# Second mixture of a pooled-attention kernel: operand sums of a later pass made ahead, first-pass stores and sums moved back

## Chip, cores and metric

The kernel runs on one core of a Trainium2 chip. The metric is the device time of one execution in microseconds (us), as the median of several runs; lower is better. Engines are named as in the profile: PE (matmul, with PEld for its weight loads), DVE (vector), ACT (scalar), POOL (GpSimd), SP (the queue that issues most DMAs).

## What is computed

Pooled attention, a routed mixture of experts (top two of eight), and a second, dense mixture. Only the last matters here; it takes the span from about 600 us to the end.

```python
def _moe2_ref(x, w_gate, w1, w2):          # x 2304x512, E = 8, F = 1024
    logits = x @ w_gate
    P = np.exp(logits - logits.max())
    for _ in range(8):
        P /= P.sum(1, keepdims=True) + 1e-09
        P /= P.sum(0, keepdims=True) + 1e-09
        P *= N / E
    for e in range(E):
        out += P[:, e:e + 1] * (np.maximum(x @ w1[e], 0.0) @ w2[e])
```

## The kernel before

Every fp32 product is three matmuls: each operand is split into a high part `h` (an ACT copy, L153) and a low part `l` (source minus high part, on DVE or POOL, L154), and h·h, h·l, l·h are summed (L148 to L150 and L1009 to L1011). `split` does one operand, `relu_split` (L158, tiles hh and hl) one that also goes through the ReLU.

The second mixture works in three passes of 768 tokens (`NPS`). A pass has 32 steps: 8 experts by 4 quarters of F. A step multiplies by blocks in a scheme with seven products instead of eight; its operands are sums of blocks. For the right operand of layer 1, the tokens, there are seven tiles per pass, `bh0` to `bh6` and `bl0` to `bl6` (B11, B21, B22, T1 to T4), each 128x768 and held once, so a new pass overwrites the tiles that the old pass read.

First pass (steps 0 to 31): `load_w` loads w1 and w2 into r1 and r2, makes four weight sums in tile `sw` (128x256 each, L174 to L177) and splits. `keep_w` stores the split weights to DRAM (`a_d`, `b_d`). `keep_t` makes four more sums of w2 in tile `tt` (L206 to L209, on POOL), splits them whole (th on ACT, tl on DVE, 128x1024) and stores them (`t_d`). It starts with the weights of step 4; the sums of steps 0 to 3 (`back`) follow in steps 10, 14, 18 and 22, with w2 loaded once more. `first2` is layer 1 (42 matmuls 128x384), `second2` layer 2 of the step before (36 matmuls 128x512), drained on DVE into `acc` (L995, L999).

In steps 2 and 3 of the first pass `balance` runs the eight normalisations of P. It is a generator: after every second product `tick` lets PE do one small matmul (L940) on column sums `bs` that DVE has just made (L938), and the order of instructions is fixed there, so PE waits if bs is late.

Passes 2 and 3 (steps 32 to 95) fetch the stored weights (`fetch_w`). `first_w` has 42 matmuls 128x384, `left_w` makes sums and splits of the hidden blocks on POOL (tiles cl), `second_w` has 63 matmuls 128x256 (L1009 to L1011), drained into `acc`: the first value of a pass ("fresh", 12 drains) by ACT with a scale (L1115), all others by DVE (L1117). `acc` is held once; when a pass is over, six DMAs take it to `out`, and the fresh drains of the next pass must wait for them.

At a change of pass `right(ps)` makes the 14 tiles in three slices of 256 columns (`right_part`): for each slice four POOL sums into `sw` (L245 to L248) and seven splits, in the order B11, T2, T3, T1, B21, T4, B22. The tokens `xr` of the last pass are loaded by `right_raw`.

A scheduler orders the instructions of each engine ahead of time; each engine then runs its list in order.

Of the kernel before, what the change touches and what calls it, by code (L numbers as in the profile page):

```python
# [8 lines left out]
F32 = mybir.dt.float32  # L9
# [19 lines left out]
def tile_pooled_attention_moe_moe(  # L29
# [46 lines left out]
    NW = 4  # L76
    G0 = PB
# [122 lines left out]
    def keep_t(r2, e, qi, pool):  # L200
# [4 lines left out]
        G = nc.gpsimd  # L205
# [4 lines left out]
        split(th, tl, t)  # L210
# [649 lines left out]
    with ExitStack() as es:  # L860
# [13 lines left out]
        XR = {}  # L874
# [84 lines left out]

        def right(ps):  # L960
            XT[ps] = right_tiles(xb, CH)
            for i in range(PB // 2):
                right_part(ps, i)

        def right_part(ps, i):
            c = i * P, (i + 1) * P
            tx = wp.tile([P, 4, K2, P], F32, name="sw", bufs=1)
            right_t(XR[ps], tx, nc.gpsimd if ps else nc.vector, *c)
            right_split(XR[ps], tx, XT[ps], *c, [nc.vector] if ps else [nc.vector, nc.gpsimd])

# [112 lines left out]
        def second_w(ps, e, qi):  # L1083
# [18 lines left out]
            for bank, l, r, again, half, cols, new in (  # L1102
# [7 lines left out]
                for t in range(h):  # L1110
# [3 lines left out]
                    if fresh and new:  # L1114
                        nc.scalar.activation(a, bank[t], AF.Copy, scale=pe)  # L1115
                    else:
                        nc.vector.scalar_tensor_tensor(a, bank[t], pe, a, op0=ALU.mult, op1=ALU.add)  # L1117
# [22 lines left out]
        back = steps[0:4]  # L1140
        for n, (ps, e, qi) in enumerate(steps):
            if n == 3:
                yg_s.close()
                tq = tq_s.enter_context(tc.tile_pool(name="tq", bufs=1, reuse_waits="tile"))
            if n + 1 < len(steps):
# [4 lines left out]
                else:  # L1150
                    W[nx] = load_w(w1b, w2b, *nx[1:], en, en)
                    if n >= 3:
                        keep_t(W[nx][4], *nx[1:], tq)
            if ps == 0:
                keep_w(W[ps, e, qi], e, qi)
                if n >= 10 and n % 4 == 2 and back:
                    st = back.pop(0)
                    r2 = wp.tile([P, FB, DM], F32, name="r2")
                    nc.sync.dma_start(r2, w2b[st[1], st[2] * QF:(st[2] + 1) * QF, :]
                                      .rearrange("(k p) d -> p k d", p=P))  # L1160
                    keep_t(r2, *st[1:], tq)
            if e == E - 1 and qi == NQ - 2 and 1 < ps + 1 < NPS:
                right_raw(ps + 1)
# [9 lines left out]
            if ps == 0:  # L1173
                first2(ps, e, qi)
                if n:
                    second2(*steps[n - 1])
                else:
# [7 lines left out]
                    for nb in range(PB, PB + 4):  # L1185
                        combine(nb)
            elif n == E * NQ:
# [41 lines left out]
```

## Time and profile before

| | |
|---|---|
| runs | 2205.8, 2208.61, 2209.41 us (median 2208.61) |
| profiled execution | 2206.33 us, its span 2204.5 us |
| granted TensorE clock | 0.975 of full speed over the span |
| PE busy | 2088.4 us (95%) |
| DVE, POOL, ACT busy | 1535.0, 1465.1, 988.6 us |
| DMA | 489.79 MB, 222 GB/s over the span |

PE's share is near full except in a few places: until about 600 us (other layers), at 720 to 790 us (the normalisations, beside steps 2 to 4 of the first pass) and at 1680 to 1740 us (the change from the second to the third pass). A window's row gives the length and, for each engine, busy us and the number of instructions, then the granted clock, the share of DMA engines busy and GB/s. A time line's row gives the start, the duration, and in brackets the idle time before it and what ended it.

### The profile page before, as it was taken

What the parts mean: (1) busy time and instruction counts of PE and PEld (TensorE: products, weight loads), DVE (VectorE), ACT (ScalarE), POOL (GpSimd) and SP (SyncE); (2) the same over time, 40 slices, a digit from 0 to 9 for tenths busy, and PEclk for the clock granted to TensorE, in tenths of its full rate; (3) what the DMA queues carried; (4) which work ended last, traced back from release to release, by engine and by line L of the source; (5) the groups of instructions that cost most, each with busy time, mean ns of one, the idle gap of its engine ahead of it and who ended that gap; (6) DMA issues with size and microseconds to landing.
All of it is one profiled execution on the core that took longest, in us unless ns stands there. A gap on an engine that the chain in (4) does not pass through costs nothing.

```text
span 2204.5 us, 35357 instructions
## 1 busy us (share of the span) xinstructions
PE 2088.4 (95%) x12801; PEld 1951.8 (89%) x12801; DVE 1535.0 (70%) x3092; ACT 988.6 (45%) x1957; POOL 1465.1 (66%) x1390
## 2 busy tenths in 40 slices
PE   4896999999999799999999999999999999999998
PEld 3785888888989688988888999999998899999998
DVE  4686777677477677777778576666767466766766
ACT  4663444454355334343434544444444544444443
POOL 3356656554371468999995767667677677677675
PEclk9788999999999899999999999999999999999999
DMA  8535343333449767888878666766666666667664
GB/s 179 156 102 146 104 144 117 123 124 110 137 168 360 247 220 285 337 320 330 327 288 312 234 236 242 254 237 245 244 241 227 224 239 256 235 237 260 237 237 163
DMA packets 182673, 489.79 MB, mean 222 GB/s; under 512 B 21312, under 2 KB 72512, under 8 KB 182368
## 3 DMA queue, kind: packets, MB, share of 16 engines
q1 hardware_dynamic: 171664, 464.73, 59.7%
q0 software_dynamic: 7664, 21.19, 2.7%
q8 instruction: 102, 1.67, 0.3%
q10 hardware_dynamic: 3168, 1.57, 0.2%
q14 instruction: 75, 0.61, 0.1%
HBM read 348.29 MB, written 139.15 MB: 221 GB/s over the span
## 4 chain that ended last, share of the span: by engine, by line
PE 64%; POOL 8%; DVE 7%; DMA 3%; issue 3%; ACT 2%; SPq 0%; POOLq 0%; ACTq 0%; DVEq 0%
PE pb L148 7%; PE pb L149 7%; PE pb L150 7%; PE py L150 4%; PE py L148 4%; PE x L1009 4%; PE py L149 4%; PE x L1010 4%; PE ph L148 4%; PE x L1011 4%; PE ph L149 3%; PE ph L150 3%; POOL al L154 3%; DVE acc L1117 2%; PE pb L1009 1%
## 5 line engine op out<-in xcount | busy, mean ns | idle before, releaser
L1117 DVE SCALAR_TENSOR_TENSOR acc<-x,Pm,acc 128x256 f32<-128x256 f32 x750 | 340.8, 478 | 110.1 <-PE x L1011 105.4
L154 POOL TENSOR_TENSOR cl<-xg,ch 128x384 fp32r<-128x384 f32 x192 | 197.4, 1028 | 258.1 <-ACT ch L153 245.4
L148 PE MATMUL pb<-bh,ah 128*128 128x384 f32 x882 | 301.1, 342 | 9.1 <-DVE acc L1117 9.0
L149 PE MATMUL pb<-bl,ah 128*128 128x384 f32 x882 | 297.8, 338 | 0.8 <-DVE bl L154 0.8
L150 PE MATMUL pb<-bh,al 128*128 128x384 f32 x882 | 296.8, 337 | 0.0
L148 PE MATMUL py<-h,hh 128*128 128x512 f32 x704 | 278.4, 396 | 5.2 <-DVE acc L999 3.8
L149 PE MATMUL py<-l,hh 128*128 128x512 f32 x704 | 277.5, 395 | 0.0
L150 PE MATMUL py<-h,hl 128*128 128x512 f32 x704 | 265.3, 397 | 3.2 <-DVE hl L158 2.8
L148 PE MATMUL ph<-bh,ah 128*128 128x384 f32 (+1 forms) x798 | 262.1, 329 | 5.1 <-DVE hl L158 3.0
L149 PE MATMUL ph<-bl,ah 128*128 128x384 f32 (+1 forms) x798 | 260.1, 326 | 0.0
L150 PE MATMUL ph<-bh,al 128*128 128x384 f32 (+1 forms) x798 | 259.3, 326 | 0.6 <-DVE al L154 0.6
L154 POOL TENSOR_TENSOR cl<-ys,ch 128x384 fp32r<-128x384 f32 x256 | 256.7, 1024 | 2.6 <-ACT ch L153 2.6
L1117 DVE SCALAR_TENSOR_TENSOR acc<-pb,Pm,acc 128x256 f32<-128x256 f32 x318 | 151.7, 478 | 83.5 <-PE pb L1011 71.8
L148 PEld LDWEIGHTS pb<-bh,ah 128*128 128x128 f32 x882 | 167.1, 189 | 16.0 <-DVE acc L1117 15.4
L999 DVE SCALAR_TENSOR_TENSOR acc<-py,Pm,acc 128x512 f32<-128x512 f32 x168 | 124.4, 745 | 66.7 <-PE py L150 65.0
L1009 PE MATMUL x<-r,ch 128*128 128x256 f32 x576 | 162.7, 285 | 7.0 <-ACT acc L1115 4.0
L149 PEld LDWEIGHTS pb<-bl,ah 128*128 128x128 f32 x882 | 167.3, 190 | 1.1 <-DVE bl L154 1.0
L150 PEld LDWEIGHTS pb<-bh,al 128*128 128x128 f32 x882 | 166.3, 189 | 0.0
L148 PEld LDWEIGHTS ph<-bh,ah 128*128 128x128 f32 x798 | 150.7, 189 | 17.0 <-DVE hl L158 4.2
L1010 PE MATMUL x<-r,ch 128*128 128x256 f32 x576 | 161.4, 282 | 0.0
L153 ACT ACTIVATE ch<-ys 128x384 fp32r<-128x384 f32 x256 | 129.4, 518 | 68.8 <-POOL ys L1068 68.6
L148 PEld LDWEIGHTS py<-h,hh 128*128 128x128 f32 x704 | 133.0, 189 | 29.8 <-DVE acc L999 6.0
(301 smaller groups left out, 5693.3 us busy)
## 6 DMA issues: line engine op xcount, KB each, us to landing
r<-in_moe_w_dram SPq DMA_DIRECT2D x148, 512.0 KB, 4.1
r<-t_d SPq DMA_DIRECT2D x128, 512.0 KB, 6.2
ah<-a_d SPq DMA_DIRECT2D x64, 896.0 KB, 4.6
al<-a_d SPq DMA_DIRECT2D x64, 896.0 KB, 7.3
a_d<-ah SPq DMA_DIRECT2D x32, 896.0 KB, 5.8
a_d<-al SPq DMA_DIRECT2D x32, 896.0 KB, 6.1
l<-b_d SPq DMA_DIRECT2D x64, 384.0 KB, 2.9
h<-b_d SPq DMA_DIRECT2D x64, 384.0 KB
```

The lines of the kernel that those rows point to most:

```text
L148: nc.tensor.matmul(ps, lh, rh, start=first, stop=False, skip_group_check=again)
L149: nc.tensor.matmul(ps, lh, rl, start=False, stop=False, skip_group_check=again)
L150: return nc.tensor.matmul(ps, ll, rh, start=False, stop=last, skip_group_check=again)
L153: nc.scalar.activation(hi, src, AF.Copy)
L154: (en or nc.vector).tensor_tensor(lo, src, hi.bitcast(F32), op=ALU.subtract)
L999: nc.vector.scalar_tensor_tensor(a, py, pe, a, op0=ALU.mult, op1=ALU.add)
L1009: nc.tensor.matmul(ps, lh, rh, start=not again, stop=False, skip_group_check=again)
L1010: nc.tensor.matmul(ps, lh, rl, start=False, stop=False, skip_group_check=again)
L1011: nc.tensor.matmul(ps, ll, rh, start=False, stop=True, skip_group_check=again)
L1117: nc.vector.scalar_tensor_tensor(a, bank[t], pe, a, op0=ALU.mult, op1=ALU.add)
```

## The change

- `right` for passes 2 and 3: three sums (128x768) are made ahead, at steps of the last expert of the pass before (`right_sum`: T1 in `sw`, T2 in `tt` or a new tile `e1`, T3 in place in `xr`); at the change itself seven whole splits 128x768 remain, in the order B11, B21, T2, T1, T3, B22, T4, with one POOL sum for T4. For the third pass the tokens are loaded, and two of the sums stand on POOL, as early as the start of the second pass.
- `keep_t` starts with the weights of step 8 (`T0` is 7). The back sums are now eight, one in each of the steps 9 to 16, after the products of the step; they run on DVE. Every `keep_t` splits in two halves of 128x512.
- `keep_w` stands behind `first2`.
- The fresh drains move from ACT to DVE (`tensor_scalar`).

The products on PE are the same 11,830 listed instructions; POOL's list gets 48 rows shorter, ACT's 36, DVE's 51 longer.

```diff
+    T0 = 7
-    def keep_t(r2, e, qi, pool):
+    def keep_t(r2, e, qi, pool, G):
...
-        G = nc.gpsimd
...
-        split(th, tl, t)
+        for c in range(0, 4, 2):
+            split(th[:, c:c + 2], tl[:, c:c + 2], t[:, c:c + 2])
...
+        def right_sum(ps, i, pool, nm):
+            G = nc.gpsimd
+            xr = XR[ps]
+            b11, b12, b22 = xr[:, 0:K2, 0, :], xr[:, 0:K2, 1, :], xr[:, K2:KD, 1, :]
...
+            if i == 0:
+                TS[ps] = [half(wp.tile([P, 4, K2, P], F32, name="sw", bufs=1))]
+                G.tensor_tensor(TS[ps][0], b12, b11, op=ALU.subtract)
+            elif i == 1:
+                TS[ps].append(half(pool.tile([P, 3 if nm == "e1" else 4, K2, P], F32, name=nm, bufs=1)))
+                G.tensor_tensor(TS[ps][1], b22, TS[ps][0], op=ALU.subtract)
+            else:
+                G.tensor_tensor(b12, b22, b12, op=ALU.subtract)
...
         def right(ps):
             XT[ps] = right_tiles(xb, CH)
-            for i in range(PB // 2):
-                right_part(ps, i)
...
+            t1, t2 = TS.pop(ps)
+            for i, src in ((B11, b11), (B21, b21), (T2, t2), (T1, t1), (T3, b12), (B22, b22)):
+                split(*XT[ps][i], src)
+                if i == B21:
+                    nc.gpsimd.tensor_tensor(b21, b21, t2, op=ALU.subtract)
+            split(*XT[ps][T4], b21)
...
-                        nc.scalar.activation(a, bank[t], AF.Copy, scale=pe)
+                        nc.vector.tensor_scalar(a, bank[t], pe, None, op0=ALU.mult)
...
-        back = steps[0:4]
+        back = steps[0:T0 + 1]
...
-                    if n >= 3:
-                        keep_t(W[nx][4], *nx[1:], tq)
-            if ps == 0:
-                keep_w(W[ps, e, qi], e, qi)
-                if n >= 10 and n % 4 == 2 and back:
...
-            if e == E - 1 and qi == NQ - 2 and 1 < ps + 1 < NPS:
-                right_raw(ps + 1)
+                    if n >= T0:
+                        keep_t(W[nx][4], *nx[1:], tq, nc.gpsimd)
...
                 first2(ps, e, qi)
                 if n:
+                    keep_w(W[ps, e, qi], e, qi)
+                if n:
                     second2(*steps[n - 1])
...
+                if n >= T0 + 2 and back:
+                    st = back.pop(0)
...
+                    keep_t(r2, *st[1:], tq, nc.vector)
...
+            if e == E - 1 and ps + 1 < NPS:
+                if qi == 0 and ps:
+                    right_raw(ps + 1)
+                elif ps and qi:
+                    right_sum(ps + 1, (0, 2, 1)[qi - 1], hc, "e1")
+                elif qi == NQ - 1:
+                    for i in range(3):
+                        right_sum(ps + 1, i, tq, "tt")
```

DVE's list around the fourth normalisation, before (cs, Pm, rs and bs belong to the normalisation; u, s, hl and acc to the step's products; line numbers as in the profile):

```order
L942 RECIPROCAL cs<-plg 128x8
L154 TENSOR_TENSOR tl<-tt,th 128x1024
L943 SCALAR_TENSOR_TENSOR Pm<-Pm,cs 128x18x8
L158 SCALAR_TENSOR_TENSOR hl<-s_7793,hh 128x384
L995 TENSOR_TENSOR acc<-py_7806,acc 128x512
L934 TENSOR_REDUCE rs<-Pm 128x18
L995 TENSOR_TENSOR acc<-py_7825,acc 128x512
L158 SCALAR_TENSOR_TENSOR hl<-u_7734,hh 128x384
L935 RECIPROCAL rs<-rs 128x18
L936 TENSOR_TENSOR Pm<-Pm,rs 128x18x8
L938 TENSOR_REDUCE bs<-Pm 128x8
```

and now (the lines of the changed file are one higher here, 23 higher from `second2` on):

```order
L943 RECIPROCAL cs<-plg 128x8
L159 SCALAR_TENSOR_TENSOR hl<-u_7702,hh 128x384
L944 SCALAR_TENSOR_TENSOR Pm<-Pm,cs 128x18x8
L935 TENSOR_REDUCE rs<-Pm 128x18
L1018 TENSOR_TENSOR acc<-py_7780,acc 128x512
L936 RECIPROCAL rs<-rs 128x18
L937 TENSOR_TENSOR Pm<-Pm,rs 128x18x8
L1018 TENSOR_TENSOR acc<-py_7799,acc 128x512
L939 TENSOR_REDUCE bs<-Pm 128x8
```

The low-part split `tl` of `keep_t` stood between the reciprocal and the multiplication; now no row of `keep_t` stands in the whole stretch of the eight normalisations.

DVE's list in one of the steps 9 to 16, now (r is the w2 tile loaded again, tt its sums):

```order
L319 TENSOR_TENSOR s_9091<-ph,u_9056 128x384
...
L155 TENSOR_TENSOR tl<-tt,th 128x512 x2
...
L206 TENSOR_TENSOR tt<-r_8989 128x256
L208 TENSOR_TENSOR tt<-r_8989 128x256
L1022 SCALAR_TENSOR_TENSOR acc<-py_9110,Pm,acc 128x512
L207 TENSOR_TENSOR tt<-r_8989,tt 128x256
L1022 SCALAR_TENSOR_TENSOR acc<-py_9118,Pm,acc 128x512
L159 SCALAR_TENSOR_TENSOR hl<-u_9056,hh 128x384
L306 TENSOR_TENSOR u_9225<-ph,m_9216 128x384
L209 TENSOR_TENSOR tt<-r_8989,tt 128x256
L155 TENSOR_TENSOR tl<-tt,th 128x512
```

Before, such a step had one `tl` row of 128x1024 and no `tt` row on DVE; now it has the four sums and two pairs of `tl` halves, between the drains that PE waits for.

DVE's list at the change to the third pass, before (a piece of it):

```order
L154 TENSOR_TENSOR bl_18698<-sw,bh_18697 128x2x128
L1117 SCALAR_TENSOR_TENSOR acc<-x_18863,Pm,acc 128x256
L1117 SCALAR_TENSOR_TENSOR acc<-x_18864,Pm,acc 128x256
L1117 SCALAR_TENSOR_TENSOR acc<-y_18865,Pm,acc 128x256
L1117 SCALAR_TENSOR_TENSOR acc<-y_18866,Pm,acc 128x256
L154 TENSOR_TENSOR bl_18694<-sw,bh_18693 128x2x128
L154 TENSOR_TENSOR bl_18692<-sw,bh_18691 128x2x128
L154 TENSOR_TENSOR bl_18690<-sw,bh_18689 128x2x128
L154 TENSOR_TENSOR bl_18698<-sw,bh_18697 128x2x128
```

and now:

```order
L155 TENSOR_TENSOR bl_18734<-sw,bh_18733 128x768
L1056 TENSOR_TENSOR u_18573<-pb_18522,u_18547 128x384
L1140 SCALAR_TENSOR_TENSOR acc<-x_18626,Pm,acc 128x256
L1140 SCALAR_TENSOR_TENSOR acc<-x_18624,Pm,acc 128x256
L155 TENSOR_TENSOR bl_18740<-xr,bh_18739 128x768
L155 TENSOR_TENSOR bl_18738<-xr,bh_18737 128x768
L1140 SCALAR_TENSOR_TENSOR acc<-pb_18622,Pm,acc 128x256
```

PE's list there, now (x_18860 is the bank whose drains end the second pass, x_19072 the same bank in the third):

```order
L1032 MATMUL x_18860<-r_18306,ch_18595 128x256
L1033 MATMUL x_18860<-r_18307,ch_18595 128x256
L1034 MATMUL x_18860<-r_18306,cl_18596 128x256
...
L1032 MATMUL x_19072<-h_18510,ch_18821 128x256
L1033 MATMUL x_19072<-l_18511,ch_18821 128x256
L1034 MATMUL x_19072<-h_18510,cl_18822 128x256
...
L1032 MATMUL x_19072<-r_18512,ch_18845 128x256
```

The 21 slice splits on DVE, four of every seven behind a POOL sum of their slice, are seven whole ones, and only the last of them waits for a sum made at the change itself. Between the last product for x_18860 and the second use of that bank in the third pass (the last row), PE's list has 27 matmuls beside the three shown. On SP four of the six DMAs to `out` now stand together ahead of the four loads of `b_d` and `t_d`, and two behind them; before, two stood ahead, two before these loads, and two behind them.

## Rows read from the trace of the kernel before

**Rows 1.** The page: busy time, and PE's busy tenths in 40 slices.

```profile
PE 2088.4 (95%) x12801; PEld 1951.8 (89%) x12801; DVE 1535.0 (70%) x3092; ACT 988.6 (45%) x1957; POOL 1465.1 (66%) x1390
PE   4896999999999799999999999999999999999998
```

**Rows 2.** Windows: a steady stretch, then the change of pass; engines PE, PEld, DVE, ACT, POOL.

```profile
1400.00:1500.00 100.00, 99.15 (x702) 98.54 (x700) 69.29 (x160) 44.14 (x92) 73.39 (x75) 1.00 0.66 239
1680.00:1720.00 40.00, 36.25 (x217) 33.12 (x216) 27.78 (x62) 17.91 (x42) 27.32 (x29) 0.96 0.58 201
1720.00:1740.00 20.00, 15.24 (x90) 14.81 (x90) 6.35 (x14) 11.50 (x26) 14.14 (x15) 0.83 0.63 247
```

**Rows 3.** Waits of PE, 1676 to 1722 us: total, times, longest.

```profile
PE pb L148 <- DVE acc L1117: 1.0, 1, 1.0
PE pb L149 <- DVE bl L154: 0.8, 1, 0.8
```

**Rows 4.** Time line of PE, SP and ACT, 1717 to 1729 us.

```profile
1717.45 0.39 PE L1009 MATMUL x<-r,ch 128*128 128x256 f32 x1
...
1719.49 1.35 SPq L1119 DMA_DIRECT2D out_dram<-acc  x2
...
1727.58 1.21 ACT L1115 ACTIVATE acc<-x,Pm 128x256 f32<-128x256 f32 x3 [2.58 <-DMA out_dram<-acc]
...
1728.11 0.58 PE L1009 MATMUL x<-r,ch 128*128 128x256 f32 x1 [3.98 <-ACT acc L1115]
```

**Rows 5.** Windows in the stretch of the normalisations.

```profile
740.00:780.00 40.00, 30.51 (x129) 25.51 (x130) 30.18 (x67) 9.07 (x14) 16.82 (x16) 0.84 0.52 191
...
764.00:768.00 4.00, 2.61 (x7) 2.25 (x8) 3.05 (x9) 0.00 (x0) 2.79 (x4) 0.50 0.93 360
768.00:772.00 4.00, 4.00 (x15) 3.19 (x14) 2.23 (x6) 0.00 (x0) 0.00 (x0) 0.72 0.01 4
```

**Rows 6.** Waits of PE, 735 to 800 us.

```profile
PE plg L940 <- DVE bs L938: 8.8, 5, 4.8
```

**Rows 7.** Time line of DVE and PE, 738 to 766 us.

```profile
738.79 1.22 DVE L154 TENSOR_TENSOR tl<-tt,th 128x1024 fp32r<-128x1024 f32 x1 [3.83 <-ACT th L153]
...
740.72 0.37 PE L920 MATMUL plg<-ident,mx 128*1 128x128 f32 x1 [0.98 <-DVE mx L918]
...
750.81 0.31 DVE L943 SCALAR_TENSOR_TENSOR Pm<-Pm,cs 128x144 f32<-128x144 f32 x1
...
757.92 1.18 DVE L154 TENSOR_TENSOR tl<-tt,th 128x1024 fp32r<-128x1024 f32 x1
759.01 1.40 DVE L943 SCALAR_TENSOR_TENSOR Pm<-Pm,cs 128x144 f32<-128x144 f32 x1
...
764.82 0.42 DVE L938 TENSOR_REDUCE bs<-Pm 128x8 f32<-128x152 f32 x1
```

**Rows 8.** Windows of 16 us (about a step), first pass; sum and mean of 19.

```profile
949.00:965.00 16.00, 16.00 (x81) 14.37 (x81) 11.08 (x17) 5.78 (x10) 14.27 (x15) 1.00 1.02 397
...
sum 304.00, PE 301.91 PEld 271.28 DVE 231.40 ACT 116.99 POOL 278.19; mean PE 15.89 PEld 14.28 DVE 12.18 ACT 6.16 POOL 14.64
```

**Rows 9.** Waits of PE and of DVE, 800 to 1210 us.

```profile
PE py L148 <- DVE acc L999: 3.4, 4, 1.6
...
DVE acc L999 <- PE py L150: 59.9, 77, 2.1
```

**Rows 10.** Tiles th and sw: DVE's operations, durations min/median/max in ns.

```profile
L154 DVE TENSOR_TENSOR tl<-tt,th x32: 1180/1359/2779, 738.8 to 1181.9; 128x1024 fp32r<-128x1024 f32 x32
...
L174 DVE TENSOR_TENSOR sw<-r x4: 416/1460/2567, 657.5 to 693.0; 128x256 f32<-128x256 f32 x4
```

**Rows 11.** Time line of DVE and POOL, 975 to 979 us.

```profile
975.99 2.42 POOL L154 TENSOR_TENSOR l<-r,h 128x1024 fp32r<-128x1024 f32 x1
...
976.19 2.62 DVE L158 SCALAR_TENSOR_TENSOR hl<-u,hh 128x384 fp32r<-128x384 f32 x1
```

**Rows 12.** Line 1115, the fresh drains on ACT.

```profile
L1115 ACT ACTIVATE acc<-x,Pm x18: 467/475/532, 1228.1 to 1739.4; 128x256 f32<-128x256 f32 x18
```

More of the change, by code (lines that the diff above doesn't have):

```diff
@@ L873, in tile_pooled_attention_moe_moe @@
         plg = ps_m.tile([P, NB, E], F32, name="plg")
-        XR = {}
+        XR, TS = {}, {}
         def right_raw(ps):
@@ L958, in tick @@
                     turn_s.enter_context(tc.issue_after(ins.ins))
+        def right_sum(ps, i, pool, nm):
+            G = nc.gpsimd
+            xr = XR[ps]
+            b11, b12, b22 = xr[:, 0:K2, 0, :], xr[:, 0:K2, 1, :], xr[:, K2:KD, 1, :]
+            half = lambda t: t.rearrange("p a k f -> p (a k f)")[:, 0:K2 * CH].rearrange("p (k n) -> p k n", k=K2)
+            if i == 0:
[6 more added lines that the diff above has]
+                G.tensor_tensor(b12, b22, b12, op=ALU.subtract)
         def right(ps):
             XT[ps] = right_tiles(xb, CH)
-            for i in range(PB // 2):
-                right_part(ps, i)
+            xr = XR[ps]
+            b11, b12, b21, b22 = xr[:, 0:K2, 0, :], xr[:, 0:K2, 1, :], xr[:, K2:KD, 0, :], xr[:, K2:KD, 1, :]
+            t1, t2 = TS.pop(ps)
[4 more added lines that the diff above has]
+            split(*XT[ps][T4], b21)
         def right_part(ps, i):
@@ L967, in right_part @@
             tx = wp.tile([P, 4, K2, P], F32, name="sw", bufs=1)
-            right_t(XR[ps], tx, nc.gpsimd if ps else nc.vector, *c)
-            right_split(XR[ps], tx, XT[ps], *c, [nc.vector] if ps else [nc.vector, nc.gpsimd])
+            right_t(XR[ps], tx, nc.vector, *c)
+            right_split(XR[ps], tx, XT[ps], *c, [nc.vector, nc.gpsimd])
         def first2(ps, e, qi):
@@ L1139, in tile_pooled_attention_moe_moe @@
         tq_s = ExitStack()
-        back = steps[0:4]
+        back = steps[0:T0 + 1]
         for n, (ps, e, qi) in enumerate(steps):
-            if n == 3:
+            if n == T0:
                 yg_s.close()
@@ L1186, in tile_pooled_attention_moe_moe @@
                         combine(nb)
+                    keep_w(W[ps, e, qi], e, qi)
+                if n >= T0 + 2 and back:
+                    st = back.pop(0)
+                    r2 = wp.tile([P, FB, DM], F32, name="r2")
+                    nc.sync.dma_start(r2, w2b[st[1], st[2] * QF:(st[2] + 1) * QF, :]
+                                      .rearrange("(k p) d -> p k d", p=P))
+                    keep_t(r2, *st[1:], tq, nc.vector)
             elif n == E * NQ:
```

5 lines of the change are left out of this document (removed).

## The prediction

> **What bounds the kernel now.** I read the page first: PE is busy for 95% of the span, and its slices show where the other 5% are [rows 1]. Outside the part ahead of the second mixture, which the change leaves alone, two places stand out: one behind 720 us and one around 1700 us. The steady row of the windows is the measure: 99.15 of 100 us busy at full clock, 702 matmuls, 0.142 us each [rows 2]. So most of the kernel is bound by PE, and PE's list of products is not shortened. The change can win only where PE is kept waiting, and can lose by making it wait anew. I then took the windows, the waits and the time lines of three stretches: the change to the third pass [rows 2 to 4], the normalisations [rows 5 to 7], and the steps of the first pass [rows 8, 9]. All sums are made against the profiled execution, 2206.33 us, which is 2.3 us below the median of the runs, 2208.61 us. About 0.2% (4.4 us) is what a measurement of this kernel can tell from no change.
>
> **Change to the third pass.** From 1680 to 1720 us PE is idle for 3.75 of 40 us, against 0.34 at the steady rate, and the clock of 0.96 costs 1.6 us more: 5.0 us lost [rows 2]. The waits are for drains and for a low part on DVE, up to 1.0 us each [rows 3]: DVE has its drains queued among 21 slice splits that wait for ACT and POOL. With the sums made ahead and seven whole splits these waits have no reason left, and I take all 5.0 us as won. The seven splits move as many elements as the 21 did, and three of the four sums stand on POOL some 450 us earlier, in a pass where POOL has 27 of 100 us free [rows 2]; I cost both at nothing. Should POOL hold up the first blocks of the second pass instead, three sums would stand there once, by size (768 columns against 1024 in 2.42 us [rows 11]) up to 5.4 us.
>
> From 1720 to 1740 us the loss is another one. PE's last product for the bank x0 is at 1717.45 us. The last two DMAs to out are issued at 1719.49 us, behind the next step's loads; ACT's first fresh drain waits for their landing until 1727.58 us, and PE goes on at 1728.11 us after 3.98 us of idleness [rows 4], with the clock down to 0.83 over the window [rows 2]. The change leaves this chain as it was: acc is still held once, the last two DMAs still stand behind the loads, and the drain waits on DVE now. From the end of that product (1717.84) to 1728.11 us are 10.3 us. Now 30 matmuls stand between the two places, at 0.142 us 4.3 us of work, so the wait is 6.0 us, 2.0 more than before. PE arrives earlier and waits longer. The two together: **3.0 us won**, between nothing (the 5.0 us end in the wait too) and 11 us (wait and slow clock go as well: 4.6 us of idleness above the steady rate and at least 1.3 us of the clock).
>
> Moving the fresh drains adds 12 operations per pass to DVE, at ACT's 0.475 us 5.7 us [rows 12]. DVE is busy for 6.35 of 20 us where they fall [rows 2], so I cost them at nothing; without that cover it would be 5.7 us per pass, twice. What is queued behind the first of them on DVE, further drains of the same step, waited for the same landing already.
>
> **Normalisations.** From 740 to 780 us PE is idle for 9.5 us, at a clock of 0.84 [rows 5]. It waits 8.8 us in five waits for bs, 4.8 us in the longest [rows 6]. In that one DVE goes through tl (1.18 us) between the reciprocal and the multiplication, which then takes 1.40 us in place of 0.31 [rows 7] beside POOL. The change has no work of keep_t left in this stretch, on DVE or POOL. I take out the tl and the stretching, 1.18 + 1.09 = 2.3 us. An earlier tl (738.79 us) stands in front of the maximum for which PE waits 0.98 us; I take this whole. Behind the long wait the clock is at 0.50 and 0.72 for 8 us: 2.61 x 0.5 + 4.00 x 0.28 = 2.4 us [rows 5], which a wait cut to 2.5 us may spare. **5.7 us won**, between 2.3 and 10 (all 8.8 us of waits and half the clock's).
>
> **Back sums and splits of the first pass.** In 800 to 1210 us PE waited 3.4 us, four times, for a drain (L999) [rows 9]; POOL's mean is 14.64 of 16 us [rows 8], and where it also has the back sums, th and tl come late and stand in front of DVE's drains. POOL loses these sums: **3.4 us won**, at least nothing. In exchange eight steps in a row get four sums and a second tl on DVE. DVE's mean is 12.18 us in 16 [rows 8], 11.9 without the four back tl that it includes. Of four sums the first took 1.46 us in the middle, from 0.42 to 2.57; I take 0.42 for the other three. A tl is 1.36 us in the middle [rows 10]. That makes 1.46 + 1.26 + 1.36 = 4.1, and 16.0 us of work in a step of 15.9: DVE is as full as POOL was in the four steps that cost 3.4 us, 0.85 each. I take the same 0.85 for each of the eight: **6.8 us lost**. The lower end is nothing (DVE waits 59.9 us for PE in these 25 steps, 2.4 each [rows 9], so there is room); the upper one is a rival below.
>
> The DMAs of such a step: loads of 1 MB, stores of 1.75 MB (a_d), 0.75 (b_d) and 1 (t_d), and for the back sums 0.5 and 1 MB more, 6 MB or 6.3 million bytes. In 15.9 us that is 396 GB/s. A window of before moved 397 GB/s with PE busy all the time [rows 8], so I take it as hidden, at the limit. On SP the stores of keep_w now stand behind first2; they are of use a pass later, and what is queued behind them is a load with a step to spare: nothing.
>
> **Sum**: -3.0 - 5.7 - 3.4 + 6.8 = -5.3 us, so 2201.0 for the profiled execution and **2203.3 us** beside the median.
>
> **Rivals.**
>
> 1. *DVE becomes the bound in steps 9 to 16* (slower). POOL works nearly all of such a step, and a DVE operation with both operands in SBUF can be held by it: hl took 2.62 us beside a POOL split of 2.42 us that had started 0.2 us before it [rows 11]. If one of the four sums takes 2.57 us and tl its longest, 2.78, the step holds 11.9 + 2.57 + 1.26 + 2.78 = 18.5 us of DVE work; PE then follows DVE, 2.6 us per step, 21 us in place of the 6.8: 2217 us. It decides as soon as DVE's work of a step passes 15.9 us for good. For it: the price of one held operation. Against it: the middle of tl is 1.36 us, so most aren't held. Chance 0.20. The Trainium skill, "SBUF — State Buffer", section "Who interferes with whom", has this as a rule: a DVE instruction with two SBUF inputs and a GpSimd one that reads SBUF share a port pair, and the later one is blocked for the whole of the other. By that rule, taken for every sum and tl, rival 1 would be the forecast; the median of tl beside a POOL that is busy for nine tenths speaks against so wide a use of it.
>
> 2. *The wait for out takes the whole gain of the pass change*: nothing won there, the rest as summed, 2206 us. For it: the chain of rows 4 is untouched. Chance 0.17.
>
> 3. *The cover in the first pass holds and the normalisations come free*: -5.0 + 2.0 - 10 - 3.4 + 0 = -16 us, 2192 us. For it: DVE's 2.4 us of waiting per step. Against it: the normalisations are a serial chain in which DVE was busy for 30 of 40 us [rows 5], little of it keep_t. Chance 0.23.
>
> 4. *The change doesn't do what it says*: with the sums hoisted, PE's list could again run ahead of the splits. PE's new list has the steady order there, so I give this 0.05, with 2208 us.
>
> **The numbers.** The forecast has 0.35; its own range is 2199 to 2208 us, from either end of the first pass's cost. Faster by over 0.2% (under 2204.2): 0.23 of rival 3, 0.22 of the forecast, 0.05 of rival 2: 0.50. Slower (over 2213): rival 1 and 0.01 of the others: 0.21. Within: the remaining 0.29. The range of 8 in 10 goes from 2190, a little below rival 3, to 2217, rival 1.
>
> **What would show it.** Right: the windows of the pass change near 39.6 of 40 us, then one wait of PE for a DVE drain of about 6 us; the longest wait for bs under 3 us; in steps 9 to 16 PE at 15.0 to 15.5 of 16, DVE close to 16. Wrong: steps 9 to 16 longer than 17 us (rival 1) or with PE full (rival 3), or new waits of PE for loads there, if the DMA rate is no longer hidden.

## The result: slower, by 1.4%

The changed kernel takes 2240.89 us in the median (2238.96 to 2245.25, four runs) against 2209.01 us; the ratio is 1.0144, with an interval of 1.0117 to 1.0170. The forecast was 2203.3 us, in a range up to 2217. The profiled execution took 2245.25 us (span 2243.5), 38.9 us more than the one of before.

Where the 39 us are is best read step by step. In each step of the second mixture DVE does one first addition (`u<-ph,m`, in later passes `u<-pb,m`); its start times make 96 marks. Between marks, in us:

```
stretch (marks)                         before   after   difference   forecast
ahead of mark 0                          667.8   672.5      +4.8           -
0 to 9    normalisations                 171.6   167.4      -4.2        -5.7
9 to 32   rest of the first pass         363.2   401.8     +38.6        +3.4
32 to 37  change to the second pass       81.4    85.1      +3.7         0
62 to 68  change to the third pass       106.1   103.6      -2.5        -3.0
0 to 95                                 1508.0  1543.6     +35.6        -5.3
```

The two gains have about the size that was forecast. The loss is nearly all in the first pass, and it doesn't end with step 16: 14.1 us are lost from mark 9 to 17, 20.6 from mark 17 to 25, and 3.8 from there to mark 32.

The changed kernel does the same work later: its normalisations come 5 us and its change to the third pass 40 to 43 us behind those of before (mark 62 is at 1704.1 us instead of 1661.2), and windows must be compared with that shift. Here are marks 0 to 9, the normalisations, the change to the third pass in two pieces, and the first pass, whole and from mark 17 on (engines PE, PEld, DVE, ACT, POOL, then the clock, the DMA share and GB/s).

```profile
672.50:839.90 167.40, 157.22 (x822) 140.00 (x821) 122.97 (x211) 70.30 (x122) 65.01 (x56) 0.96 0.70 256
745.00:785.00 40.00, 31.91 (x141) 26.43 (x142) 30.93 (x71) 7.70 (x13) 10.06 (x8) 0.90 0.35 126
...
1720.00:1760.00 40.00, 37.08 (x240) 35.63 (x238) 29.68 (x58) 19.19 (x37) 30.37 (x28) 0.96 0.64 220
1760.00:1780.00 20.00, 15.54 (x86) 15.12 (x87) 10.65 (x25) 6.54 (x13) 10.71 (x11) 0.83 0.56 197
...
840.00:1241.70 401.70, 374.97 (x1791) 327.77 (x1790) 345.91 (x444) 149.62 (x268) 308.91 (x263) 0.98 0.83 302
977.60:1241.70 264.10, 246.13 (x1170) 216.68 (x1169) 222.79 (x284) 97.56 (x174) 205.66 (x175) 0.97 0.82 299
```

Of the kernel before, marks 0 to 9 and the first pass, whole and the same 15 steps:

```profile
667.80:839.40 171.60, 158.80 (x824) 141.87 (x823) 130.37 (x214) 73.99 (x124) 81.69 (x74) 0.94 0.75 273
839.40:1202.50 363.10, 359.28 (x1785) 321.55 (x1784) 276.25 (x389) 140.26 (x245) 317.85 (x284) 1.00 0.85 315
962.90:1202.50 239.60, 235.78 (x1167) 210.26 (x1166) 182.58 (x260) 92.55 (x164) 208.49 (x185) 1.00 0.85 312
```

In the last 15 steps PE does the same matmuls in both, DVE is busy for 40 us more, and PE idles for 18 us, at a clock of 0.97, where it idled for 4. What PE waits for in the first pass of the changed kernel (marks 9 to 32; total, times, longest), which answers to [rows 9]:

```profile
PE py L149 <- DVE acc L1022: 15.5, 16, 2.1
PE ph L149 <- DVE hl L159: 3.8, 5, 1.9
PE ph L149 <- DVE u L306: 3.7, 3, 3.1
PE ph L149 <- DVE u L313: 2.6, 1, 2.6
PE ph L149 <- DVE u L310: 1.0, 2, 0.7
```

All 26.6 us are for DVE; before it was 3.8. So waits are 23 of the 38.6 us lost. The granted clock over the stretch, 1.00 before and 0.98 now, is some 8 us more (an estimate, 0.02 of 402 us), and the rest isn't split further here. The third view says why DVE is late: two of its costliest groups from mark 17 to 32 of the changed kernel (busy, mean ns of one, then idle time before), and the one group that answers to it in the kernel before.

```profile
L155 DVE TENSOR_TENSOR tl<-tt,th 128x512 fp32r<-128x512 f32 x40 | 54.8, 1390 | 3.5 <-ACT th L154 3.5
L159 DVE SCALAR_TENSOR_TENSOR hl<-u,hh 128x384 fp32r<-128x384 f32 x30 | 35.3, 1175 | 0.1
```

```profile
L154 DVE TENSOR_TENSOR tl<-tt,th 128x1024 fp32r<-128x1024 f32 x17 | 29.0, 1707 | 7.1 <-ACT th L153 6.8
```

A half costs 1.39 us, nearly as much as a whole one of twice the size (1.71). And there are 40 halves, for 20 sets of sums, where 17 whole ones stood before: sets whose place in the program is ahead of step 17 are executed behind it.

### The profile page after: what moved, and what is told of

The parts are those of the page before. It is cut to its first block, busy times and chain, and to the rows that moved or that the text cites. A ratio compares the mean times of both kernels' runs of the same rounds, so it can differ in the third digit from the quotient of the medians.

```text
span 2243.5 us, 35330 instructions
## 1 busy us (share of the span) xinstructions
PE 2101.1 (94%) x12801; PEld 1956.6 (87%) x12801; DVE 1602.5 (71%) x3152; ACT 982.9 (44%) x1937; POOL 1434.4 (64%) x1342
## 4 chain that ended last, share of the span: by engine, by line
PE 66%; DVE 10%; DMA 4%; POOL 3%; issue 2%; ACT 1%; SPq 0%; DVEq 0%; POOLq 0%; ACTq 0%
PE pb L149 7%; PE pb L150 7%; PE pb L151 7%; PE py L151 4%; PE py L149 4%; PE py L150 4%; PE ph L149 4%; PE x L1032 4%; PE x L1033 4%; PE ph L150 4%; PE ph L151 4%; PE x L1034 4%; DVE hl L159 2%; DVE acc L1140 2%; PE pb L1032 1%
## 5 line engine op out<-in xcount | busy, mean ns | idle before, releaser
L149 PE MATMUL pb<-bh,ah 128*128 128x384 f32 x882 | 301.6, 342 | 10.2 <-DVE acc L1140 10.0
L149 PEld LDWEIGHTS pb<-bh,ah 128*128 128x128 f32 x882 | 167.8, 190 | 16.5 <-DVE acc L1140 16.1
L150 PEld LDWEIGHTS ph<-bl,ah 128*128 128x128 f32 x798 | 151.7, 190 | 9.0
```

The lines of the kernel that those rows point to most:

```text
L149: nc.tensor.matmul(ps, lh, rh, start=first, stop=False, skip_group_check=again)
L150: nc.tensor.matmul(ps, lh, rl, start=False, stop=False, skip_group_check=again)
```

## The experiments

The part ahead of mark 0, which no experiment touches, took 667 to 697 us from one set of runs to the next, so the kernel before itself was at 2205 to 2233 us; each kernel is judged by its ratio to the runs of before on the same chip, and by its own marks. The table of all of them stands at the end of this section.

### Which part of the change is it?

The first three runs undo one part of the change each, the fourth undoes all parts of the first pass.

**e1_whole**

```diff
-        for c in range(0, 4, 2):
-            split(th[:, c:c + 2], tl[:, c:c + 2], t[:, c:c + 2])
+        split(th, tl, t)
```

> The changed kernel with keep_t's splits whole again (128x1024), all else as changed. Theory H: each half of tl waits behind a POOL operation as long as the whole one did (1.21 us in the middle for 128x512 against 1.36 for 128x1024), so DVE has about 1 us more per step of the first pass; whole splits give back 15 to 25 us of the 32, most of it in steps 17 to 31: 2216 to 2226 us. Theory B (the sums on DVE in steps 9 to 16 are the whole cause, and the later steps only inherit their disorder): at most 5 us, 2236 us or more. Theory K (the stores of keep_w, moved behind first2, hold up the loads on SP): no change, 2241 us.

Measured: 1.0120 (1.0097 to 1.0143), 5 us less than the changed kernel by the ratio, with intervals that overlap, and 400.4 us from mark 9 to 32 instead of 401.8. That is what theory B gave, but its reason, that DVE's sums are the whole cause, doesn't hold, as the next runs show.

**e3_keepw**

```diff
+            if ps == 0:
+                keep_w(W[ps, e, qi], e, qi)
...
                 first2(ps, e, qi)
                 if n:
-                    keep_w(W[ps, e, qi], e, qi)
-                if n:
                     second2(*steps[n - 1])
```

> The changed kernel with keep_w ahead of first2 again, all else as changed. Theory K: gives back 15 to 25 us, 2216 to 2226 us, with the loads of w1 and w2 issued earlier in a step. Theories H and B: within 5 us of the changed kernel, 2236 to 2246 us.

Measured: 1.0133 (1.0113 to 1.0153), 400.0 us from mark 9 to 32. Theory K falls.

**e4_pool**

```diff
-                    keep_t(r2, *st[1:], tq, nc.vector)
+                    keep_t(r2, *st[1:], tq, nc.gpsimd)
```

> The changed kernel with the eight back sums on POOL instead of DVE, still one step each in steps 9 to 16. Theory B: steps 9 to 16 fall from 18 us to about 16.8 (POOL full, 0.85 us lost per step as in the four such steps before), 10 us less, 2231 us. Theory H: the halves still block, DVE loses only 2.7 us of work per step: 5 to 8 us less. Theory K: no change.

Measured: 1.0103 (1.0084 to 1.0122), 394.5 us: 7 us less there and 9 by the ratio, which doesn't decide between theories B and H. It took as long as the changed kernel from mark 17 to 32 (265.1 us against 264.1), so the loss there doesn't need the sums on DVE.

**e6_whole_t3_keepw** (the edits of e1 and e3, and this one)

```diff
-    T0 = 7
+    T0 = 3
...
+            if ps == 0 and n >= 10 and n % 4 == 2 and back:
+                st = back.pop(0)
...
+                keep_t(r2, *st[1:], tq, nc.gpsimd)
```

> The first pass as before (whole splits, keep_t from step 4, four back sums on POOL, keep_w ahead of first2); of the change only right, its sums made ahead and the fresh drains on DVE are left. If the whole loss comes from the first pass's steps: the normalisations cost what they did before (5 us lost again), the change to the second pass costs the 4 us that the trace of the changed kernel shows or, if those were owed to the disorder before it, none, and the change to the third pass gives 3 us: 2206 to 2211 us. A rival, that the sums made ahead or the drains on DVE are themselves the cause: 2225 us or more.

Measured: 0.9989 (0.9975 to 1.0003), 364.8 us from mark 9 to 32, PE's waits for DVE 4.3 us. The whole loss is in the first pass's steps. Undoing one of three parts took back 2 to 9 us of 32; undoing these three and a fourth, the late start with eight sets in a row, took back all. So none of the three is the cause alone. The fourth was not undone by itself.

### Each part alone

So the next runs put one part back on top of e6.

**e5_k_alone** (e6 without the edit of e3)

> e6 with one part of the change put back: keep_w behind first2. Between the changed kernel and e6 lie four parts of the first pass, and undoing any one of three took back at most a quarter; this asks what each does alone. Theory 'sum of parts' (each part adds its own delay, DVE's work per step above all): keep_w adds no work, so within 5 us of e6 (ratio to before 0.997 to 1.001). Theory 'convoy' (what hurts is the order on SP and ACT: stores and splits that wait stand in front of the next weights): 10 us or more above e6, ratio 1.003 or more.

Measured: 0.9984 (0.9971 to 0.9997), 363.5 us. The place of keep_w costs nothing.

**h_alone** (e6 without the edit of e1)

> e6 with one part put back: th and tl in halves. In the changed kernel's steps 17 to 31 a half took 1.39 us on DVE, a whole one 1.71 in the kernel before, so halves cost DVE about 1.1 us per step, 31 us over 28 steps, of which DVE's waiting for PE (35 us in those 15 steps before) can take up much. Theory H: 10 to 20 us above e6, ratio 1.003 to 1.008. Theory 'sum of parts' with enough cover while nothing else is added: 0 to 5 us, ratio up to 1.001.

Measured: 1.0048 (1.0031 to 1.0064), 376.2 us from mark 9 to 32: 11 us above e6. PE's waits there:

```profile
PE py L149 <- DVE acc L1022: 9.7, 10, 1.9
PE ph L149 <- DVE hl L159: 1.0, 1, 1.0
```

Halves alone make PE wait 6.4 us more for DVE. This part the prediction had not costed at all.

**t_alone** (e6 with T0 = 7 and eight back sums, behind the products of steps 9 to 16, on POOL)

> e6 with one part put back: keep_t from step 8 and eight back sums, one per step in steps 9 to 16 behind the products, on POOL. The normalisations become as fast as in the changed kernel (5 us won against e6). Theory W (the back sums use the same two buffers for w2 as the loads, so each step's next load of w2 waits until the sums have been read: SP waited 43 us for them in e4_pool, 16 us in e6): 10 to 20 us lost in the steps from 9 on, ratio 1.001 to 1.006. Theory D (POOL or DVE full only in steps 9 to 16): 8 x 0.85 = 7 us lost there and none behind, ratio about 1.000. Either way less than the changed kernel.

Measured: 1.0074 (1.0046 to 1.0102), 381.9 us: 17 us above e6, though its first 9 marks were as fast as e6's or faster. Theory W had the right size for the wrong reason: in the next run SP waited nearly as long for the same buffers (38 us against 45), and nothing was lost.

**v1_every3** (whole splits, keep_w ahead of first2, T0 = 7)

```diff
+            if ps == 0 and n >= 10 and n % 3 == 1 and back:
+                st = back.pop(0)
...
+                keep_t(r2, *st[1:], tq, nc.gpsimd)
```

> e6 with keep_t from step 8, and the eight back sums on POOL every third step from 10 to 31, ahead of the products as in the kernel before. Meant to keep what won: the normalisations' 5 us and the third pass's 2 to 3 us. If spacing lets the buffers and POOL recover (four such steps cost 3.4 us before, so eight cost 7): e6 less 5 plus 3, ratio 0.998. If a step with back sums costs what it did in e4_pool, ratio 1.002 or more.

Measured: 0.9985 (0.9972 to 0.9997), 365.1 us: eight sets cost 0.3 us more than the four of e6. What t_alone and v1 do in the same stretch of time, in this order:

```profile
861.00:1053.00 192.00, 180.93 (x890) 159.36 (x889) 142.31 (x184) 72.55 (x120) 178.22 (x164) 1.00 0.88 325
```

```profile
861.00:1053.00 192.00, 189.54 (x945) 170.07 (x944) 147.74 (x199) 75.60 (x128) 177.75 (x158) 1.00 0.88 327
```

POOL is busy for 178 of 192 us in both, and executes 17 sets in t_alone against 16: it has about the same work, and yet PE gets 8.6 us less done. What differs besides is the order of PE's own list: in t_alone, where eight sets in a row stand in POOL's list, the scheduler moves PE's products. F is a run of layer 1's matmuls in PE's list, S one of layer 2's, with their number (counted from the lists; a bar parts steps):

```
v1        S6 F6 S6 F12 S12 F12 S12 F12 | S6 F6 S6 F12 S12 F12 S12 F12 | ...
t_alone   S12 F18 S12 F12 S12 F18 S2 F12 S10 F12 S12 F12 S12 F24 S2 F18 S10 F12 S12 F6 S12 F42 S2 F12 S10
changed   S12 F18 S12 F12 S12 F30 S2 F18 S10 F12 S12 F12 S12 F18 S2 F12 S10 F6 S12 F6 S12 F6 S12 F12 S12
```

F6 is one of the seven products, S6 one drain of layer 2. The even rhythm is gone for about ten steps: F42 is a step's whole layer 1 at once, whose additions and splits then come to DVE in a row, with no layer 2 between. e1, e4 and the changed kernel have such a stretch too. v1 keeps the rhythm throughout; e6, dve2, h_alone and v3_halves (below) nearly so, with no run of F over 18, as in the kernel before. PE's waits from mark 9 to 32 fit this. Of t_alone's 16.5 us for DVE, 9.3 are for hl, u and s, the sums and splits of layer 1's products:

```profile
PE py L149 <- DVE acc L1021: 7.2, 11, 1.3
PE ph L149 <- DVE hl L159: 5.9, 4, 2.5
```

v1 waits for drains alone:

```profile
PE py L149 <- DVE acc L1021: 6.0, 5, 1.6
```

In the changed kernel the first run of F over 18, the F30, starts at 1003.4 us, behind mark 18. The 14.1 us up to mark 17 were lost while the order was still nearly even; the 20.6 us behind it fall in the broken stretch.

### Density, place and engine

**v1_behind** (v1 with the sums behind the step's products)

> v1 (eight back sums on POOL, every third step from 10 to 31, whole splits) with the back sums behind the step's products, where the change has them, instead of ahead of them. t_alone lost 19 us in the first pass's steps, v1 only 1; they differ in density (each step against every third) and in place. Theory density (POOL has 14 us of work in a step of 16, the sums bring 3.5 more, so eight steps in a row pile up a backlog, and a step with two ordinary ones behind it doesn't): as v1, ratio 0.997 to 1.000. Theory place: as t_alone, ratio 1.005 or more.

Measured: 0.9999 (0.9987 to 1.0011), 368.7 us. Place costs about 3 us, by the ratio and by the marks, near the least that they can tell; it is the density in the program that costs, and that breaks the order. That the broken order is how it costs is argued from t_alone against v1, not shown: a kernel with t_alone's sets in v1's order of products wasn't tried, and dve2 below loses as much with the order nearly even.

**v1_dve3**

```diff
-                keep_t(r2, *st[1:], tq, nc.gpsimd)
+                keep_t(r2, *st[1:], tq, nc.vector)
```

> v1 with the back sums on DVE, every third step. In the changed kernel DVE's share was the larger part of the loss. Theory density (it is DVE without a pause to catch up): PE loses 1 to 4 us in these steps as in v1, ratio 0.997 to 1.000. Theory 'sums on DVE hurt as such' (each of them blocked behind POOL in front of a drain that PE waits for): 8 x 2 us as in steps 9 to 16 of the changed kernel, ratio 1.005 or more.

Measured: 0.9988 (0.9976 to 1.0000), PE's waits for DVE 3.4 us. Sums on DVE cost nothing that shows, if DVE has two steps to recover.

**dve2** (v1_dve3 with `n >= 9 and n % 2 == 1`)

> v1_dve3 with the sums every second step (9 to 23) instead of every third. Theory density with a threshold (a step without sums has 4 us of DVE free, enough for one step's backlog): as v1_dve3, ratio 0.998 to 1.000, PE's loss in the first pass 2 to 6 us. Theory 'loss in proportion to density': half of the changed kernel's loss, 10 us or more, ratio 1.003 or more.

Measured: 1.0061 (1.0043 to 1.0079), 382.4 us from mark 9 to 32, 15.4 us of PE's waits for DVE. One free step per set, which I had expected to do, is too little; two are enough. Yet DVE's mean is only 14.0 us per step here against 13.1 in v1_dve3, in a step of 15.9.

**v3_halves** (v3_dve3_acc, below, with th and tl in halves)

> v3 with th and tl in halves. h_alone lost 10 us with four back sums on POOL. Theory H (each half waits for POOL about as long as a whole one, so DVE has 1 us more in each step, in front of a drain): 8 to 14 us above v3, ratio 1.000 to 1.003. Rival (halves hurt only where POOL has the back sums too): within 3 us of v3.

Measured: 0.9996 (0.9983 to 1.0010) against v3's 0.9956, and 379.9 us against 363.3. Halves cost 9 to 17 us with POOL free of the back sums too; the rival falls.

### The wait for out, and a better version

**before_acc** (the kernel before)

```diff
-                AC[ps] = ra.tile([P, PB, DM], F32, name="acc", bufs=1)
+                AC[ps] = [ra.tile([P, DM], F32, name=f"acc{i}", bufs=1) for i in range(PB)]
...
-                a = AC[ps][:, i, :]
+                a = AC[ps][i]
```

> The kernel before with acc as six tiles, one per 128 tokens, instead of one, nothing else changed. A fresh drain then waits for the DMA to out of its own 128 tokens alone. If the wait at the change to the third pass is the last pair of DMAs behind the next step's loads, it goes: 4.0 us of idleness and the slow clock behind it, 5 to 7 us less, ratio 0.997. If the clock falls there anyway or another wait takes the place: ratio 0.999 to 1.001.

Measured: 0.9995 (0.9984 to 1.0006): not to be told from no change. The wait of 3.98 us [rows 4] is gone, and the time from mark 62 to 68 is 103.0 us instead of 106.1, but the slice splits make new waits:

```profile
PE x L1009 <- DVE acc L1117: 2.2, 3, 1.4
PE pb L148 <- ACT bh L153: 2.1, 1, 2.1
PE x L1011 <- POOL cl L154: 1.1, 1, 1.1
```

**v2_acc** (v1 with the six tiles)

> v1 with acc as six tiles. Meant as the better version: v1's gains (normalisations 4 to 5 us, change of pass 2 us) and the wait for out removed at the change to the third pass (6.0 us of loss there in v1, 2 to 3 us at most of it left): ratio 0.9945 to 0.997. If the wait is taken over by another (weights not there, cl late): ratio 0.998 to 0.999.

Measured: 0.9976 (0.9963 to 0.9988), mark 62 to 68 in 96.1 us. Whole splits gave 2.5 us alone and six tiles 3.1 alone; together they give 10. Each takes away the wait that the other leaves.

**v3_dve3_acc** (v1_dve3 with the six tiles)

> v1_dve3 (sums on DVE every third step, which lost less in the first pass than v1) with acc as six tiles (which took 7 us of loss from v1 at the change to the third pass). If the two gains add: 2.7 + 7 us under the kernel before's time, ratio 0.994 to 0.997. If they don't (noise between chips and runs is 0.1%): as v2_acc, 0.9976.

Measured: **0.9956** (0.9940 to 0.9973), the fastest of all beside v4: 0.44% under the kernel before, 1.9% under the changed one by the ratios. The longest of its waits of PE at the change to the third pass (1670 to 1790 us):

```profile
PE pb L149 <- DVE acc L1139: 2.0, 4, 0.9
PE y L1031 <- ACT ch L154: 0.8, 2, 0.4
PE x L1031 <- DVE acc L1139: 0.6, 1, 0.6
```

**v4_slices1** (v3 with the second pass's operands in slices again, their sums at the change)

> v3 with the right operands of the second pass made as before, in slices with the sums at the change; only the third pass has its sums ahead. The change to the second pass loses 1.5 to 3 us in every kernel with the whole splits, none in before_acc. Theory: the whole splits and the early sums for the third pass stand in front of the first fresh drains; then 1 to 3 us less than v3, ratio 0.993 to 0.996. Rival: the loss comes from the fresh drains on DVE, which stay: as v3.

Measured: 0.9957 (0.9941 to 0.9973). From mark 32 to 37 it takes 80.2 us against 81.5 in v3, and PE's waits there, 2.0 us in v3, are gone, as its theory says. The whole kernel is no faster: from mark 0 to 32 it takes 537.1 us against v3's 532.5, though the program differs there in the last step alone.

**v3_act** (v3 with the fresh drains on ACT)

> v3 with the fresh drains on ACT again, as before the change. The prediction took their move to DVE at nothing. If so: as v3, ratio 0.994 to 0.997, and the wait at the change to the third pass the same. If it was their move that freed the change of pass: 2 us or more above v3, ratio 0.997 or more.

Measured: 0.9976 (0.9958 to 0.9995); from mark 0 to 95 it took 1498.6 us against v3's 1496.9, and 94.8 against 94.3 from mark 62 to 68. The intervals overlap. The drains' engine is worth 2 us at most in the trace, and whether the 0.2% of the ratios are more than the part ahead of mark 0 stays open.

All marks together; "waits" are PE's for DVE from mark 9 to 32, DVE is its mean busy time per step there, in us:

```
kernel        ratio   0-9    9-32   waits  DVE    32-37  62-68   0-95
before        1       171.6  363.2   3.8   12.0   81.4   106.1  1508.0
after         1.0144  167.4  401.8  26.6   15.0   85.1   103.6  1543.6
e1_whole      1.0120  168.8  400.4  27.1   14.3   84.9   103.4  1542.9
e3_keepw      1.0133  167.4  400.0  25.3   15.0   83.3   101.5  1537.9
e4_pool       1.0103  166.2  394.5  21.4   13.8   83.2   101.4  1530.9
e6            0.9989  172.1  364.8   4.3   12.1   82.8   103.2  1508.8
e5_k_alone    0.9984  171.2  363.5   3.7   12.7   82.0   101.9  1505.5
h_alone       1.0048  169.1  376.2  10.7   12.9   82.0   103.0  1516.5
t_alone       1.0074  171.2  381.9  16.5   12.7   82.9   103.6  1525.2
v1_every3     0.9985  169.1  365.1   6.0   12.3   82.7   103.1  1507.8
v1_behind     0.9999  168.9  368.7   6.1   12.4   82.8   102.9  1511.3
v1_dve3       0.9988  165.2  366.5   3.4   13.1   82.5   101.3  1503.6
dve2          1.0061  169.1  382.4  15.4   14.0   83.0   102.6  1524.3
v3_halves     0.9996  166.1  379.9  13.8   13.6   82.0    94.8  1510.6
before_acc    0.9995  170.5  362.8   3.7   12.0   80.2   103.0  1504.6
v2_acc        0.9976  165.5  369.8   6.6   12.4   82.8    96.1  1503.1
v3_dve3_acc   0.9956  169.2  363.3   2.9   13.1   81.5    94.3  1496.9
v4_slices1    0.9957  165.5  371.6   6.7   13.3   80.2    94.7  1500.1
v3_act        0.9976  168.7  364.7   4.0   13.1   83.4    94.8  1498.6
```

Single marks are good to some 4 us, since the order of products around a mark differs between kernels; the last column is not touched by that. v3 and v4 tell what differences up to 5 us are worth: their first passes differ in the last step alone.

## Why the prediction was wrong

**The step that failed is the cost of the first pass**, "eight steps in a row get four sums and a second tl on DVE", 6.8 us lost against 3.4 won. The stretch lost 38.6 us. Three things were wrong in it.

First, its extent and the price of the halves. It costed steps 9 to 16 and their second set alone, and said of the halves nothing: two halves were taken as one whole tl of 1.36 us. But the halves are in every step. They cost 11 us alone (h_alone against e6; 13 by the ratio). How, the time line shows; DVE first, then POOL, in the changed kernel, at a step that has no back sums of its own on DVE:

```profile
1061.80 0.75 DVE L1022 SCALAR_TENSOR_TENSOR acc<-py,Pm,acc 128x512 f32<-128x512 f32 x1 [1.87 <-PE py L151]
1062.59 2.23 DVE L155 TENSOR_TENSOR tl<-tt,th 128x512 fp32r<-128x512 f32 x1
1064.74 0.74 DVE L1022 SCALAR_TENSOR_TENSOR acc<-py,Pm,acc 128x512 f32<-128x512 f32 x1
1065.40 2.18 DVE L155 TENSOR_TENSOR tl<-tt,th 128x512 fp32r<-128x512 f32 x1
1067.51 1.07 DVE L159 SCALAR_TENSOR_TENSOR hl<-u,hh 128x384 fp32r<-128x384 f32 x1
1068.50 0.55 DVE L306 TENSOR_TENSOR u<-ph,m 128x384 f32<-128x384 f32 x1
```

```profile
1061.85 2.42 POOL L155 TENSOR_TENSOR al<-sw,ah 128x1024 fp32r<-128x1024 f32 x1
1064.21 2.83 POOL L155 TENSOR_TENSOR l<-r,h 128x1024 fp32r<-128x1024 f32 x1
```

Each half starts inside a POOL split of 128x1024 and ends about half a microsecond behind it. PE's idle time at that place is 1.10 us for the drain at 1064.74 and 3.06 us for the addition at 1068.50, which reads PSUM and has a normal 0.55 us itself, but stands behind the two halves and hl:

```profile
1065.54 0.50 PE L149 MATMUL py<-h,hh 128*128 128x512 f32 x1 [1.10 <-DVE acc L1022]
...
1069.10 0.69 PE L149 MATMUL ph<-bh,ah 128*128 128x384 f32 x1 [3.06 <-DVE u L306]
```

The Trainium skill, "SBUF — State Buffer", section "Who interferes with whom", gives the rule: a DVE instruction with two SBUF inputs waits for the end of a GpSimd one that reads SBUF and started first. The trace agrees: tl is blocked, while the drain between the halves (one SBUF operand, one in PSUM) took its usual 0.74 us beside the same POOL split. The prediction weighed that rule and turned it down by the median of the whole tl (1.36 us against at least 1.18). That row holds for one long operation. Cut in two, it waits twice: a half took at least 0.67 us and 1.21 in the middle over the whole pass. The rule's form of the argument, a price per instruction and not per byte, would have been the better one here.

Second, the price of a full engine. The prediction took 0.85 us per step from the four steps of before where POOL was full, as if the list around the sets stayed as it was. It read the new place of the sums from DVE's list, but not what became of PE's: the products of ten steps were listed in another rhythm. t_alone, which moves no sum to DVE, lost 17 us to e6; spread over every third step, the same eight sets leave the rhythm as it was and cost nothing that shows on either engine (v1_every3, v1_dve3). That shows the price of the density; that it is paid by way of the rhythm fits PE's waits and remains argued. Every second step on DVE keeps the rhythm and costs 16 us all the same (dve2 against v1_dve3), so a free step between is not enough.

Third, the measure of a full DVE. The prediction compared DVE's work of a step, 16.0 us, with the step's length. From mark 9 to 17 DVE was busy for 123.1 us of 137.6, 15.4 per step of 17.2, and PE lost 14.1 us all the same:

```profile
840.00:977.60 137.60, 128.84 (x623) 111.10 (x622) 123.12 (x161) 52.07 (x94) 103.25 (x89) 1.00 0.85 307
```

The sums on DVE took up to 2.6 us, and 0.42 to 0.96 in the middle (tile tt of the changed kernel, min/median/max in ns):

```profile
L206 DVE TENSOR_TENSOR tt<-r x8: 409/494/1505, 860.9 to 1028.0; 128x256 f32<-128x256 f32 x8
L208 DVE TENSOR_TENSOR tt<-r x8: 422/960/2622, 861.3 to 1028.4; 128x256 f32<-128x256 f32 x8
L207 DVE TENSOR_TENSOR tt<-r,tt x8: 410/688/2591, 862.2 to 1029.3; 128x256 f32<-128x256 f32 x8
L209 DVE TENSOR_TENSOR tt<-r,tt x8: 407/418/962, 863.0 to 1030.8; 128x256 f32<-128x256 f32 x8
```

The four medians make 2.6 us, and I had 2.7; their size was right. The last set on DVE runs at 1028 us, behind mark 20; its place in the program is step 16. **Rival 1** named the right engine and side, and its sign came, steps of over 17 us (17.2). Its condition, more than 15.9 us of DVE's work in a step, did not, and its price of 21 us for steps 9 to 16 was above what the changed kernel lost from mark 9 to 17 (14.1 us); with the range's end put on it, the 24 us behind mark 17 fell outside. The three parts don't add: they are 11 us (halves alone), 17 (eight sets in a row on POOL alone) and, from t_alone to e1_whole, 18 more for moving the sums to DVE, where keep_w's place, which differs too, is taken as free; the sum, 47, stands against 37 us between e6 and the changed kernel (401.8 - 364.8).

**Normalisations: right**, 4.2 us won of 5.7 forecast: PE's idle time from mark 0 to 9 fell from 12.8 to 10.2 us, and its busy time, with the same products, by 1.6. From mark 0 to 6 the kernels with keep_t from step 8 took 123 to 127 us, those with it from step 4 127 to 129. The longest wait for bs is 3.0 us:

```profile
PE plg L941 <- DVE bs L939: 6.6, 6, 3.0
...
PE plg L921 <- DVE mx L919: 0.8, 1, 0.8
```

Those were 4.8 and 0.98 us [rows 6, 7]. The two waits were to give 3.3 us, all waits gave 2.6. The clock was to give 2.4; it went from 0.94 to 0.96 between the marks, and the 1.6 us of busy time are put down to it.

**Change to the third pass: the size by luck**, 2.5 us for 3.0, for neither term came as summed. Ahead of the wait for out 5.0 us were to be won, as the waits for DVE had "no reason left". The window from 1720 us, which answers to the one from 1680 before [rows 2], has PE busy for 37.08 of 40 us instead of 36.25, not for 39.6, and the clock is 0.96 as before. So 0.8 us were won there. The longest wait left is for a drain that stands behind a whole split on DVE; the last two rows are PE's:

```profile
1725.47 2.38 DVE L155 TENSOR_TENSOR bl<-xr,bh 128x768 fp32r<-128x768 f32 x1
1727.77 0.47 DVE L1140 SCALAR_TENSOR_TENSOR acc<-pb,Pm,acc 128x256 f32<-128x256 f32 x1
...
1767.26 1.27 DVE L1138 TENSOR_SCALAR acc<-x,Pm 128x256 f32<-128x256 f32 x3 [5.34 <-DMA out_dram<-acc]
```

```profile
1728.30 0.44 PE L149 MATMUL pb<-bh,ah 128*128 128x384 f32 x1 [1.79 <-DVE acc L1140]
...
1767.80 0.58 PE L1032 MATMUL x<-r,ch 128*128 128x256 f32 x1 [4.23 <-DVE acc L1138]
```

The wait for out, with the fresh drains now on DVE, was to grow by 2.0 us to 6.0; it is 4.23 us, 0.25 more than before. The two together make 0.6 us, not 3.0. PE's idle time between marks 62 and 68 fell by 1.1 us (8.8 to 7.7); what makes up the rest of the 2.5 is open, so that the sum came near is luck.

Rival 2, that the wait takes the whole gain, is borne out in part: with acc in one tile the kernels with whole splits win 2.5 to 4.8 us from mark 62 to 68, with six tiles 10 to 12.

**Change to the second pass: a small miss**. I had costed it at nothing; it lost 3.7 us here, 0.1 to 3.5 in the experiments with whole splits, and nothing where the second pass's operands were left in slices (v4_slices1). Here 2.2 us are one wait of PE for a fresh drain on DVE, another term that I had put at nothing; but with the drains on ACT again the place was no faster (83.4 us in v3_act). The wait:

```profile
1268.02 0.39 PE L1032 MATMUL x<-r,ch 128*128 128x256 f32 x1 [2.23 <-DVE acc L1138]
```

**DMA and keep_w: right**. e5_k_alone put a price of nothing on keep_w's place. In no run did PE wait from mark 9 to 32 for anything but DVE for more than 0.2 us in all.

## What to carry to other kernels

Before giving extra work to an engine whose results the bottleneck drains, count instructions that can be blocked, not bytes alone: an operation cut in two can wait twice, and each wait stands in front of a drain. Work that must be made up is best spread with free steps between; the same eight sets cost nothing that shows every third step and 17 us or more in a row. Where a scheduler sets the order, read what the change does to the list of the engine that bounds the kernel, even if its instructions are the same ones. When undoing single parts recovers little, don't conclude that they are harmless: undo all, then put each back alone. And compare windows of two kernels by their place in the work and not by their time: 40 us lost ahead of a place shift all that is behind it.

## What was not expected

- A 128x512 subtraction on DVE took 0.67 to 2.90 us in the first pass, 1.21 in the middle, beside a POOL that is busy for 309 of 402 us; the ACT copy of the same halves kept to 0.61 to 0.64 us:

```profile
L154 ACT ACTIVATE th<-tt x64: 613/632/636, 810.3 to 1220.8; 128x512 fp32r<-128x512 f32 x64
L155 DVE TENSOR_TENSOR tl<-tt,th x64: 673/1206/2904, 811.0 to 1225.0; 128x512 fp32r<-128x512 f32 x64
```

- PE waited 14 to 15 us for DVE in kernels where DVE was busy for 13.6 and 14.0 us per step on the mean and PE's order was as before (v3_halves, dve2), and 3.4 us where it was 13.1 (v1_dve3). The time line above suggests why: what counts is the row of blocked operations between two drains.
- Two waits at one place, each removed alone, were worth 2.5 and 3.1 us, and 10 to 12 together (v2_acc, v3_dve3_acc against before, marks 62 to 68). In v3 some 5 us of that are the clock (an estimate, 0.05 of 106 us), which is at 1.00 there; before and v3:

```profile
1661.20:1767.40 106.20, 97.41 (x630) 93.49 (x629) 67.90 (x153) 52.76 (x118) 74.43 (x76) 0.95 0.62 226
```

```profile
1690.20:1784.60 94.40, 91.07 (x629) 89.30 (x628) 69.25 (x152) 45.95 (x91) 69.12 (x66) 1.00 0.70 248
```
